# An accuracy check moved from steps 4–9 to steps 11–15 of the first blocks, and a row-placing product with four matmuls in place of eight

## The chip, the cores and the metric

One NeuronCore of a Trainium2 chip runs the whole kernel in one launch. The metric is device time in microseconds (us) of that core. Five engines work side by side, each through its own list of instructions in the order of the program: TensorE (PE; its weight loads are shown apart as PEld), VectorE (DVE), ScalarE (ACT), GpSimd (POOL) and SyncE (SP), which here only issues transfers. An instruction that has to wait for another engine holds up everything behind it on its own engine.

## The reference

The output is the sum of the input, a Fourier mixing and a token-mixing MLP, both fed by a layer norm:

```python
xn = _layernorm(x, axis=-1)
return x + _A_ref(xn, dft_seq_re, dft_seq_im, dft_hid_re, dft_hid_im) + _B_ref(xn, w1, b1, w2, b2)
# A: y = Cr @ (xn @ Dr^T) - Ci @ (xn @ Di^T)      Cr, Ci 2048x2048; Dr, Di 640x640
# B: u = gelu(h^T @ w1 + b1), y = (u @ w2 + b2)^T  h = layernorm(xn); w1 2048x1728, w2 1728x2048
```

There are 2048 tokens and 640 channels, all in float32. The Fourier matrices come as inputs; the kernel uses their symmetries to read and multiply only a part of them, so it also has to check that the matrices it was given have these symmetries. If a check fails, a general branch at the end computes everything again.

## The kernel before

**Arithmetic.** A float32 operand is split into a high part (rounded, written by ACT, function `high`, line 130) and a low part (what is left, written by DVE, function `low`, line 133). A product is then three matmuls: high by high, high by low, low by high (function `three`, lines 138 to 140). Nearly all matmuls move 320 columns against 128x128 weights.

**Steps.** The program is a list of steps, each with about 24 matmuls of 320 columns. At each step `i` the final loop (lines 1329 to 1343) emits, in this order: the loads of step `i`, the reads of finished sums, the high part of the weight piece of step `i+2`, the work in the list `middle`, the low part of that piece, the work in the list `behind`, and last the matmuls of step `i`. Since the order is written by hand (`tc.manual_schedule()`), this is the order on each engine.

**The first blocks** are steps 0 to 15 (`n_first = 16`). Step `j` multiplies one block of 128 tokens (a row of x, normalized) by the four weight pieces of its group; sums for the first four blocks of hidden features collect in all eight PSUM banks (line 301). For each row of x there is a chain that runs through three engines: moments on DVE (lines 200, 203), a reciprocal root `q` on ACT (line 225), four small operations on POOL (lines 229 to 232, tiles `r` and `again`), the normalized row on ACT (tile `zt`, line 245), its high part on ACT (tile `x`, line 130) and its low part on DVE (tile `x`, line 133). In steps 4 to 11 ACT and DVE also cut the weight pieces 8 to 15 (tile `early`).

**Around step 16.** In step 14 DVE writes the low part of the last row, then four 0/1 matrices (`places_compare`, lines 415 and 417), then the low part of the weight piece of step 16 (tile `piece`). In step 15 ACT cuts the piece of step 17, computes `q_all` (line 398) and loads the table for gelu (line 1161); DVE computes the factors of all rows (lines 399 to 402), splits them (`norm_parts`, tile `norm_cut`), checks two scales (`scale_check`, lines 1103 to 1107) and writes the low part of the piece of step 17. At the head of step 16 ACT reads the eight banks with gelu (line 325, eight instructions, banks 0 and 1 first). The matmuls of step 16 write into banks 0 and 1 and cannot begin before these were read.

**The check sets.** A set (`seq_set`, `set_at`) loads four pieces of 512 KB of the sequence matrices: a base and three ends. Three ends are compared with the base on DVE (end 1: line 999; end 2: line 1003 twice; end 3: line 1005 twice) and the base with its own mirror image (line 1012). Each of the four differences is squared and summed on ACT right after it (line 1022, `measure`, which for early sets is emitted with the compare). The list `when` holds the steps of the four loads; a compare follows its load by `by` steps, in the list `behind`. Seven sets are early (they load through SP); the first of them is the one that moves. Its loads stand at steps 4, 4, 5, 6 and its compares at steps 7, 8 and 9. Its base lies in the tile `ck0`, which `scale_load` (lines 1097 and 1098, step 10) also uses; its ends lie in the memory of the tiles `n6` and `n7`, which later hold the last four rows of x.

**The factors' places.** Step 17 ends with `norm_products`: 0/1 matrices bring the factors of the rows, their high and low part one after the other, into the order that the Fourier part wants (line 429, eight matmuls of 32 columns into bank 6). In step 18 `norm_places` copies the sums with ACT (line 436) into `ck1`, and POOL spreads them (lines 443 to 448) into `norm_pairs`, first used in step 20 (line 470).

Of the kernel before, what the change touches and what calls it, by code (L numbers as in the profile page):

```python
# [8 lines left out]
F32 = mybir.dt.float32  # L9
# [3 lines left out]
AF = mybir.ActivationFunctionType  # L13
# [3 lines left out]
P = 128  # L17
S = 2048
D = 640
F = 1728  # L20
NS = S // P
# [28 lines left out]
def fnet_plus_mixer(  # L50
# [22 lines left out]
    nc = tc.nc  # L73

    keep = ctx.enter_context(tc.tile_pool(name="keep", bufs=1))
# [28 lines left out]
    norm_cut = keep.tile([P, 2, NS, 2], R32, name="norm_cut")  # L104
# [18 lines left out]
    psum = [acc.tile([P, CH], F32, name=f"psum{i}") for i in range(8)]  # L123
    idle = nc.const_aps.tensor(1.0, [P, CH], dtype=BF16)
    for i in range(WARM):
        n = CH if i < WARM - 8 else P // 2
# [18 lines left out]
    def at(i, f, *args, when=middle):  # L145
        when[i].append(lambda: f(*args))
# [188 lines left out]
    for f, g in up_order:  # L335

        def products(w, f=f, g=g):
            for k in range(g * G, (g + 1) * G):
                up_products(f, k, w, up_banks[f])
            if (f, g) == (FIRST, 1):  # L340
                norm_products()

        at(len(steps) - 6, w1_load, f, g, when=loads)
        top, bottom = cut_view(lambda a: a[:, :CH], lambda f=f, g=g: w_at[f, g])

        def beside(top=top, f=f, g=g):
            hi = top_tiles[f, g]
            pieces = [a.rearrange("p (k t) -> p k t", k=G)[:, :, TAIL:] for a in (hi, w_at[f, g])]
            low(pieces[0], pieces[1], pieces[0])
            return hi, hi  # L350

        def top_beside(f=f, g=g):
            top_tiles[f, g] = cut_tile()[:, 0, :CH]
            high(top_tiles[f, g], w_at[f, g])

        steps.append(((top, bottom) if f < NF else (top_beside, beside)) + (products,))
        if g == NG - 1 and f < NF:
            at(len(steps) + (f == NFB - 2), gelu, f, when=reads)
# [60 lines left out]
    lanes_of, places = [], []  # L419
# [3 lines left out]
        low(norm_cut[:, 1], norm, norm_cut[:, 0])  # L423

    def norm_products():
        n = 2 * NS
        for c in range(4):
            for part in range(2):
                nc.tensor.matmul(
                    psum[6][:, c * n : (c + 1) * n], places[0][:, c // 2, c % 2], norm_cut[:, part].rearrange("p k c -> p (k c)"),  # L430
                    start=c == 0 and part == 0, stop=c == 3 and part == 1, skip_group_check=True,
                )

    def norm_places():
        of = ck[1][:, : 8 * NS]
        nc.scalar.activation(of, psum[6][:, : 8 * NS], AF.Copy)
        of = of.rearrange("p (s v h k c) -> p s v h k c", s=2, v=2, h=2, k=HS)
        to = norm_pairs.rearrange("p (h b j v) c -> p b v h j c", h=2, b=2, v=2)
        half = P // 2
        for v in range(2):  # L440
            for i in range(2):
                p = slice(half * i, half * (i + 1))
                nc.gpsimd.tensor_copy(to[p, 0, v], of[p, 0, v, :, i : i + 2 * NJ - 1 : 2])

            nc.gpsimd.tensor_copy(to[:, 1, v], of[:, 1, v, :, HS - 2 : HS - 1 - 2 * NJ : -2])
            p = slice(0, half + 1 - v)
            nc.gpsimd.tensor_copy(to[p, 1, v], of[p, 1, v, :, HS - 1 : HS - 2 * NJ : -2])
        nc.gpsimd.tensor_copy(to[0:1, 1, 0], of[0:1, 1, 0, :, NK : NK + 2 * NJ - 1 : 2])
# [582 lines left out]
    def set_at(u, when, by, base, places, late):  # L1031
        load, compare, compare_mirror = seq_set(u, base, places, late)
        for i in range(len(when)):
            at(when[i], load, i, when=loads)
            if i:
                at(when[i] + by, compare, i, when[i] + by, when=behind)
        at(when[-1] + by, compare_mirror, when[-1] + by, when=behind)
# [88 lines left out]
    n_first = len(k_order)  # L1126
# [24 lines left out]
    at(n_first - 2, places_compare)  # L1151
    at(n_first - 1, norm_parts)
    at(n_first + 2, norm_places)
    for j in range(NJ):
        for h in range(2):
# [6 lines left out]
    for k in range(HS):  # L1162
        i = n_first + 3 + 4 * k
# [6 lines left out]
    i = n_first + 3 + 4 * NK  # L1170
# [8 lines left out]
    sets = [m * HS + k for m in range(2) for k in range(NG, HS)] + [m * HS + k for m in range(2) for k in range(NG)]  # L1179

    def early_base(n):
        return lambda: ck[(n + 1) % 2][:, : S // 2]
# [4 lines left out]
        return keep.tile([P, S // 2], F32, name=f"check{n}", tag=f"h{4 + i}")  # L1187


    first_ends = []  # L1190

    def first_place(i):
        if i != 1:
            first_ends.append(keep.tile([P, 2, S // 2], F32, name=f"check_first{i}", tag=f"n{6 + i // 2}"))
        return first_ends[-1][:, i % 2]

    set_at(sets[0], [4, 4, 5, 6], 3, early_base(1), first_place, 0)
    for n in range(1, n_early):
        i = n_first + 4 * (n - 1)
        when = [i, i, i + 1, i + 2] if n < n_early - 1 else [i, i, i + 1, i + 4]  # L1200
# [20 lines left out]
    for n in range(n_hid_units):  # L1221
        load, compare, compare_own, measure = hid_unit(n)
        i = begin + 4 + 8 * n
# [256 lines left out]
```

## Time and profile before

| what | value |
|---|---|
| median of 3 runs | 439.84 us (439.14 to 439.93) |
| the profiled execution | 439.92 us, span of its instructions 438.1 us |
| TensorE busy | 430.7 us, 98% of the span, 2963 matmuls |
| VectorE busy | 326.1 us, 74% |
| ScalarE busy | 247.1 us, 56% |
| GpSimd busy | 108.6 us, 25% |
| mean granted TensorE clock | 0.997 |
| HBM | 94.58 MB read, 10.49 MB written |

The span runs from the first instruction to the last. What lies between 438.1 and 439.92 us is outside the instructions. A row of the timeline gives start and duration in us, the engine, the line of the kernel, the operation, the tile written and the tiles read, and in square brackets how long the engine sat idle before and what ended it. Ends of matmuls are modelled: a matmul of 320 columns is drawn 0.31 us long, while the next one starts after some 0.15 us.

### The profile page before, as it was taken

The page shows a single profiled execution, that of the slowest core. Times are in us where ns is not written, and L with a number is a line of the kernel's source. Part 1 is how long each engine was busy: PE and PEld are TensorE (multiplying, and loading weights), DVE is VectorE, ACT ScalarE, POOL GpSimd, SP SyncE. Part 2 cuts the span into 40 slices and gives each one's busy share as a digit, 9 for nine tenths or more (in the row PEclk, how much of TensorE's full clock was granted, in tenths as well). Part 3 has the DMA queues.
Part 4 walks back from the last instruction along what each step waited for, and adds up shares of the span by engine and source line. Part 5 has one row for each costly group of instructions (what it writes and reads, how often), then busy time and mean ns, then how long its engine had stood idle before and what let it go on. Part 6 is the DMA issues. An engine that isn't in the chain of part 4 may idle for free.

```text
span 438.1 us, 8076 instructions
## 1 busy us (share of the span) xinstructions
PE 430.7 (98%) x2963; PEld 424.4 (97%) x2963; DVE 326.1 (74%) x665; ACT 247.1 (56%) x476; POOL 108.6 (25%) x164
## 2 busy tenths in 40 slices
PE   9999999999999999999999999999999999999994
PEld 5999999999999999999999999999999999999994
DVE  7887861578777777795888759989778677869671
ACT  5967955566556646475946424556645555545540
POOL 2056511032220001100002425546434516312000
PEclk9999999999999999999999999999999999999998
DMA  8992347597886561233203799999999988996301
GB/s 271 339 373 101 104 180 272 178 322 269 279 287 226 194 222 57 72 99 95 101 23 122 212 339 397 389 396 364 404 402 399 399 315 287 407 328 240 113 31 38
DMA packets 43839, 105.68 MB, mean 241 GB/s; under 512 B 5748, under 2 KB 7940, under 8 KB 43792
## 3 DMA queue, kind: packets, MB, share of 16 engines
q1 hardware_dynamic: 34816, 72.66, 46.5%
q0 software_dynamic: 8832, 32.27, 20.2%
q8 instruction: 25, 0.41, 0.4%
q14 instruction: 22, 0.18, 0.1%
q10 hardware_dynamic: 144, 0.16, 0.1%
HBM read 94.58 MB, written 10.49 MB: 240 GB/s over the span
## 4 chain that ended last, share of the span: by engine, by line
PE 87%; DMA 3%; DVE 3%; ACT 2%; POOL 2%; issue 1%; SPq 1%; POOLq 0%; ACTq 0%
PE psum L138 26%; PE psum L140 26%; PE psum L139 26%; PE psum L301 4%; PE psum L897 2%; PE psum L290 2%; DMA xp<-in_x 1%; ACT zt L245 1%; DMA xm<-in_x 1%; POOL r L230 1%; DVE st L200 1%; DVE x L133 1%; DVE early L133 0%; SPq L1258 0%; ACT x L130 0%
## 5 line engine op out<-in xcount | busy, mean ns | idle before, releaser
L133 DVE TENSOR_TENSOR piece<-w_raw,piece 128x512 fp32r<-128x512 f32 (+2 forms) x128 | 76.5, 598 | 80.3 <-ACT piece L130 75.6
L130 ACT ACTIVATE piece<-w_raw 128x512 fp32r<-128x512 f32 (+2 forms) x112 | 67.0, 600 | 110.1 <-PE psum L140 73.4
L138 PE MATMUL psum<-x,piece 128*128 128x320 f32 x288 | 89.1, 309 | 0.0
L140 PE MATMUL psum<-x,piece 128*128 128x320 f32 x288 | 89.1, 309 | 0.0
L139 PE MATMUL psum<-x,piece 128*128 128x320 f32 x288 | 88.8, 308 | 0.0
L1022 ACT ACTIVATE check<-check 128x1024 f32<-128x1024 f32 (+2 forms) x62 | 61.4, 991 | 32.5 <-DVE check L1005 14.2
L140 PE MATMUL psum<-h_cut,piece 128*128 128x320 f32 x256 | 79.2, 310 | 0.0
L138 PE MATMUL psum<-h_cut,piece 128*128 128x320 f32 x256 | 79.1, 309 | 0.0
L139 PE MATMUL psum<-h_cut,piece 128*128 128x320 f32 x256 | 78.8, 308 | 0.0
L301 PE MATMUL psum<-x,early 128*128 128x320 f32 x384 | 58.5, 312 | 1.1 <-DVE x L133 0.4
L301 PEld LDWEIGHTS psum<-x,early 128*128 128x128 f32 x384 | 56.4, 188 | 3.1 <-ACT x L130 1.2
L138 PEld LDWEIGHTS psum<-x,piece 128*128 128x128 f32 x288 | 54.1, 188 | 0.0
L139 PEld LDWEIGHTS psum<-x,piece 128*128 128x128 f32 x288 | 54.1, 188 | 0.0
L140 PEld LDWEIGHTS psum<-x,piece 128*128 128x128 f32 x288 | 54.1, 188 | 0.0
L138 PE MATMUL psum<-h_high,piece 128*128 128x320 f32 x160 | 49.6, 310 | 0.0
L139 PE MATMUL psum<-h_low,piece 128*128 128x320 f32 x160 | 49.4, 309 | 0.0
L140 PE MATMUL psum<-h_high,piece 128*128 128x320 f32 x160 | 49.3, 308 | 0.0
L139 PEld LDWEIGHTS psum<-h_cut,piece 128*128 128x128 f32 x256 | 48.1, 188 | 0.0
L140 PEld LDWEIGHTS psum<-h_cut,piece 128*128 128x128 f32 x256 | 48.1, 188 | 0.0
L138 PEld LDWEIGHTS psum<-h_cut,piece 128*128 128x128 f32 x256 | 48.1, 188 | 0.0
L991 POOL DMA_DIRECT2D check<-in_dft_seq x36 | 26.6, 744 | 16.8 <-ACT check L1022 15.5
L984 POOL DMA_INDIRECT check<-in_dft_seq,from_seq x16 | 19.1, 1191 | 44.8 <-ACT check L1022 41.8
(235 smaller groups left out, 781.7 us busy)
## 6 DMA issues: line engine op xcount, KB each, us to landing
check<-in_dft_seq POOLq DMA_DIRECT2D x36, 512.0 KB
w_raw<-in_w SPq DMA_DIRECT2D x56, 256.0 KB
check<-in_dft_seq SPq DMA_DIRECT2D x18, 512.0 KB
w_raw<-in_w SPq DMA_DIRECT2D x16, 512.0 KB
w_raw<-in_w SPq DMA_DIRECT2D x16, 384.0 KB
rest<-y SPq DMA_DIRECT2D x16, 320.0 KB
rest<-in_x SPq DMA_DIRECT2D x16, 320.0 KB
out<-rest SPq DMA_DIRECT2D x15, 320.0 KB
```

What stands on the lines that cost most here:

```text
L130: nc.scalar.activation(hi, src, AF.Copy)
L133: nc.vector.tensor_sub(lo, src, hi.bitcast(F32))
L138: nc.tensor.matmul(bank, wh, mh, start=first, stop=False, skip_group_check=True)
L139: nc.tensor.matmul(bank, wh, ml, start=False, stop=False, skip_group_check=True)
L140: nc.tensor.matmul(bank, wl, mh, start=False, stop=last, skip_group_check=True)
L200: nc.vector.bn_stats(stats[k][:, i, :], rows[k][:, i * H2 : (i + 1) * H2])
L290: nc.tensor.matmul(to[half][:, :H2], w[0][:, c], m[i], start=k == to[2] and i == 0, stop=k == to[3] and i == 1, skip_group_check=True,)
L301: nc.tensor.matmul(up_banks[f][half][:, :H2], w_cut[f, k // G][part == 2][:, c], n[:, part == 1, k % 2, half * H2 : (half + 1) * H2], star ...
L897: nc.tensor.matmul(to, w[0][:, c], m[which], start=False, stop=last and which == 1, skip_group_check=True,)
L984: nc.gpsimd.indirect_dma_start(to[:, c * CH : (c + 1) * CH], None, dft_seq.rearrange("c k p t -> (c k p) t"), bass.IndirectOffsetOnAxis(ap ...
L991: (nc.gpsimd if late else nc.sync).dma_start(to.rearrange("p (c t) -> p c t", c=2), dft_seq[c : c + 2, k + HS * (i // 2)].rearrange("c p t ...
L1022: nc.scalar.activation(v, v, AF.Square, accum_out=off[:, n : n + 1])
```

## The change

The check set that ran in steps 4 to 9 now loads in steps 11, 12, 12 and 13 (`n_first - 5`, `- 4`, `- 4`, `- 3`) and compares two steps later: ends 1 and 2 in step 14, end 3 and the mirror in step 15. Its base lies in `ck1` instead of `ck0`, its ends in the memory of `h0`, `h1` and `h2`, which until step 11 hold the weight pieces 8, 9 and 10 and after step 16 the outputs of gelu. In `norm_products` the high and low parts lie side by side, so that four matmuls of 64 columns do what eight of 32 did, and the sum of the two parts, which TensorE formed before by adding into the same columns, is formed in `norm_places`: ACT copies the low sums, and DVE adds the high sums to them.

```diff
     def norm_products():
-        n = 2 * NS
+        n = 4 * NS
         for c in range(4):
-            for part in range(2):
-                nc.tensor.matmul(
-                    psum[6][:, c * n : (c + 1) * n], places[0][:, c // 2, c % 2], norm_cut[:, part].rearrange("p k c -> p (k c)"),
-                    start=c == 0 and part == 0, stop=c == 3 and part == 1, skip_group_check=True,
-                )
+            nc.tensor.matmul(
+                psum[6][:, c * n : (c + 1) * n], places[0][:, c // 2, c % 2], norm_cut.rearrange("p i k c -> p (i k c)"),
+                start=c == 0, stop=c == 3, skip_group_check=True,
+            )
 
     def norm_places():
         of = ck[1][:, : 8 * NS]
-        nc.scalar.activation(of, psum[6][:, : 8 * NS], AF.Copy)
+        both = psum[6][:, : 16 * NS].rearrange("p (s i n) -> p i s n", s=4, i=2)
+        sums = of.rearrange("p (s n) -> p s n", s=4)
+        nc.scalar.activation(sums, both[:, 1], AF.Copy)
+        nc.vector.tensor_add(sums, both[:, 0], sums)
...
-    first_ends = []
-
     def first_place(i):
-        if i != 1:
-            first_ends.append(keep.tile([P, 2, S // 2], F32, name=f"check_first{i}", tag=f"n{6 + i // 2}"))
-        return first_ends[-1][:, i % 2]
-
-    set_at(sets[0], [4, 4, 5, 6], 3, early_base(1), first_place, 0)
+        return keep.tile([P, S // 2], F32, name="check_first", tag=f"h{i}")
+
+    set_at(sets[0], [n_first - 5, n_first - 4, n_first - 4, n_first - 3], 2, early_base(0), first_place, 0)
```

## The prediction

> **What bounds the kernel now.** I read the page first, for the share of each engine and the chain that ended last:
>
> ```profile
> PE 430.7 (98%) x2963; PEld 424.4 (97%) x2963; DVE 326.1 (74%) x665; ACT 247.1 (56%) x476; POOL 108.6 (25%) x164
> PE 87%; DMA 3%; DVE 3%; ACT 2%; POOL 2%; issue 1%; SPq 1%; POOLq 0%; ACTq 0%
> ```
>
> TensorE is the bound. So a change can do two things: shorten TensorE's list, or shorten or lengthen its gaps. Next I read TensorE's own timeline, for the gaps:
>
> ```profile
> 40.36 0.56 PE L301 MATMUL psum<-x,early 128*128 128x320 f32 x2 [0.18 <-DVE early L133]
> 41.26 8.48 PE L301 MATMUL psum<-x,early 128*128 128x320 f32 x56 [0.34 <-ACT x L130]
> 50.12 16.69 PE L301 MATMUL psum<-x,early 128*128 128x320 f32 x112 [0.38 <-DVE x L133]
> 66.65 0.31 PE L138 MATMUL psum<-x,piece 128*128 128x320 f32 x1
> ```
>
> From 50.12 to 66.65 run 112 matmuls without a gap, 0.148 us each; the last of these rows is the first matmul of step 16. At this pace the gaps ahead of the first three rows cost 0.18 + 0.31 - 0.15 = 0.34 us (the drawn end is 0.31 after a start), 0.90 - 0.30 = 0.60 (two matmuls take 0.90) and 8.86 - 8.27 = 0.59 (56 matmuls take 8.86): **1.53 us** in steps 8 to 11. The list of waits shows no gap of TensorE behind a work engine after that.
>
> Then the timeline of the other engines around these gaps:
>
> ```profile
> 33.02 0.28 ACT L225 ACTIVATE q<-mv,eps 128x1 f32<-128x1 f32 x1
> 34.95 0.92 ACT L245 ACTIVATE zt<-xp,again 128x640 f32<-128x640 f32 x1 [1.13 <-POOL again L232]
> ...
> 36.55 0.28 ACT L225 ACTIVATE q<-mv,eps 128x1 f32<-128x1 f32 x1
> 37.00 1.76 POOL L230 TENSOR_SCALAR r<-r,q 128x1 f32<-128x1 f32 x1 [1.37 <-ACT q L225]
> 37.42 1.29 DVE L999 SCALAR_TENSOR_TENSOR check_first<-ck,parity,check_first 128x1024 f32<-128x1024 f32 x1
> 39.52 0.92 ACT L245 ACTIVATE zt<-xp,again 128x640 f32<-128x640 f32 x1 [1.99 <-POOL again L232]
> ...
> 41.12 1.05 ACT L1022 ACTIVATE check_first<-check_first 128x1024 f32<-128x1024 f32 x1
> 41.99 1.29 DVE L1003 TENSOR_TENSOR check_first<-ck,check_first 128x512 f32<-128x512 f32 x2
> 42.16 0.62 ACT L130 ACTIVATE early<-w_raw 128x512 fp32r<-128x512 f32 x1
> ...
> 45.53 1.41 DVE L1005 SCALAR_TENSOR_TENSOR check_first<-ck,parity,check_first 128x512 f32<-128x512 f32 x2
> 46.98 0.75 DVE L1012 SCALAR_TENSOR_TENSOR ck<-ck,parity 128x512 f32<-128x512 f32 x1
> ...
> 48.82 0.62 ACT L1022 ACTIVATE ck<-ck 128x512 f32<-128x512 f32 x1
> ...
> 50.14 0.91 ACT L245 ACTIVATE zt<-xm,again 128x640 f32<-128x640 f32 x1
> ```
>
> The old place of the check makes those gaps. GpSimd's line 230 ends at 38.76, just as VectorE's compare of end 1 ends at 38.71, so the root-to-row path takes 39.52 - 36.55 = 2.97 us against 34.95 - 33.02 = 1.93 one row earlier: 1.04 us late. After that ScalarE's squares and VectorE's compares stand in the rows' chains.
>
> Last, the stretch in which the check lands:
>
> ```profile
> 58.51 1.14 ACT L130 ACTIVATE piece<-w_raw 128x512 fp32r<-128x512 f32 x2
> 59.38 0.22 DVE L415 TENSOR_SCALAR lane<-lane 128x128 int32<-128x128 int32 x1
> 59.55 0.29 ACT L398 ACTIVATE q_all<-mv,eps 128x16 f32<-128x16 f32 x1
> 59.86 1.28 ACT L1161 ACT_TABLE_LOAD   x1
> 60.51 0.68 DVE L133 TENSOR_TENSOR piece<-w_raw,piece 128x512 fp32r<-128x512 f32 x1
> 61.12 0.17 DVE L399 SCALAR_TENSOR_TENSOR r_all<-mv,q_all 128x16 f32<-128x16 f32 x1
> 63.98 0.67 DVE L133 TENSOR_TENSOR piece<-w_raw,piece 128x512 fp32r<-128x512 f32 x1
> 65.83 3.46 ACT L325 ACTIVATE h<-psum,b_sb 128x320 f32<-128x320 f32 x8 [4.47 <-PE psum L301]
> ```
>
> ScalarE waits 4.47 us for TensorE before the gelu reads, then TensorE starts step 16 0.82 us after the first of them begins. There is no slack on TensorE's side: if ScalarE is not free when step 15 ends, step 16 starts late and all that follows with it.
>
> **The check leaves steps 7 to 9.** TensorE's 1.53 us would go, so that step 16 could start at 66.65 - 1.53 = 65.12. The rows gain more. The row of 39.52 comes at 36.55 + 1.93 = 38.48, 1.04 us earlier. The three squares of the ends (42.16 - 41.12 = 1.04 each) and that of the mirror (0.62) leave ScalarE, another 3.74, and the ScalarE rows from 39.52 to 50.14 show no wait for anything else. So the row of 50.14 comes 4.78 us earlier, at 45.36. GpSimd hardly limits this: its factors must be there at 45.36, and its own chain, some 1.9 us after a root (as above), is shorter than ScalarE's 2.3 us a row ((10.62 - 3.74) / 3). From there to 59.38 nothing of the old check is left, so I move it as a block: VectorE reaches the 0/1 matrices at 59.38 - 4.78 = **54.60**.
>
> **The check arrives in steps 14 and 15.** I follow the hand-written order. VectorE: matrices 1.13 (60.51 - 59.38), low piece 0.61 (61.12 - 60.51), so end 1 begins at 56.34; end 1 takes 1.29 and end 2 1.29, to 58.92. ScalarE may not cut the piece of step 17 before it has squared end 2: 1.04, to 59.96; the piece 0.52 (half of 59.55 - 58.51), `q_all` 0.29, to 60.77. VectorE waits 1.85 us for that, since its next work needs `q_all`. Then come factors, split and scale check, 2.86 (63.98 - 61.12), the low piece 0.67, end 3 1.41: 65.71. ScalarE squares end 3 (1.04) and the mirror (0.62; the mirror's 0.75 on VectorE lies beside the square): **67.37**. The table load of 1.28 lies in ScalarE's wait. Only then gelu reads bank 0. Eight reads in 3.46 are 0.43 apart, and the start of step 16 lay 0.82 behind the first where TensorE set it; I take 0.60, between. Step 16 starts at 67.97 in place of 66.65: **+1.32 us**, though 65.12 was open to TensorE. The old wait goes, and a later one of 2.85 us comes; behind the gelu reads on ScalarE stand the pieces of steps 18 and 19, not due before 75.
>
> Bounds: drawn durations overlap a little (the piece of 60.51 lasts 0.68, its follower starts after 0.61), over eight instructions up to 0.6 us earlier; the hand-over may be 0.17 shorter (one read) or 0.22 longer (0.82); GpSimd may hold a row up by some 0.5. So +0.5 to +2.0.
>
> **Its four loads** of 512 KB leave SP's steps 4 to 6. No gap names a transfer there, so their leaving counts nothing; it cannot cost. In the new place ends 1 and 2 wait on SP until TensorE has left the weight pieces 8 and 9, near the end of step 11 (65.12 less four steps of 24 x 0.148 is 50.95; say 50.3). Queued behind them are the pieces of step 19 and later and the first pair loads, not due for 15 us.
>
> ```profile
> 49.83 1.77 SPq L267 DMA_DIRECT2D w_raw<-in_w  x4
> 51.50:52.00 0.50, 1.00 1.05 397
> ```
>
> Transfers issued at 49.83 flow in full (397 GB/s, last number of the window's row) 1.7 us later; 0.52 MB then take 1.3. Ends 1 and 2 land near 53.3 and 54.7, before 56.34 and 57.63: no cost. Only if they landed over 2.9 us later would the check slip by the rest. `scale_load` no longer waits for the base, since that is now `ck1`; nothing waited for it.
>
> **The factors' places.** TensorE first:
>
> ```profile
> 73.54 0.31 PE L140 MATMUL psum<-x,piece 128*128 128x320 f32 x1
> 73.68 0.96 PE L429 MATMUL psum<-norm_cut,places_of 128*128 128x32 f32 x8
> ...
> 74.72 0.31 PE L139 MATMUL psum<-x,piece 128*128 128x320 f32 x1
> ...
> 221.47 0.27 PE L139 MATMUL psum<-hid_main,t 128*128 128x162 f32 x1
> ...
> 222.03 0.35 PE L138 MATMUL psum<-hid_mix,t 128*128 128x324 f32 x1
> ```
>
> Between 73.54 and 74.72 lie the eight and two common matmuls: 1.18 - 0.30 = 0.88, or 0.11 each. From 221.47 to 222.03 five matmuls of 162 columns start, also 0.11 each. So 32 and 162 columns cost the same here, and 64 lie between: four instead of eight save **0.44** (0.40 to 0.48 with the rounding of the starts). In step 18 one copy on ScalarE stays a copy, and VectorE gets an addition that waits for it:
>
> ```profile
> 74.59 0.69 DVE L133 TENSOR_TENSOR piece<-w_raw,piece 128x512 fp32r<-128x512 f32 x1 [2.87 <-ACT piece L130]
> 74.68 0.28 ACT L436 ACTIVATE ck<-psum 128x128 f32<-128x128 f32 x1
> ```
>
> Queued behind the addition is the low part of step 20's piece, which now begins at 74.59. It waits for a copy that starts at 74.68 and an addition of 128 columns, which lasts between nothing and the 0.69 of the 512 columns above: at most 1.1 us later, and TensorE wants it two steps, 7.1 us, after. GpSimd's copies move by the addition too; their result is first used in step 20. I cost it at nothing.
>
> **Sum.** 439.92 (the profiled execution, 0.08 above the median of the runs) + 1.32 - 0.44 = **440.80 us**, with its own range 440.0 to 441.5. The gaps taken out of steps 8 to 11 come back, larger, in front of step 16.
>
> **The gap and the clock.** In the forecast TensorE idles from about 65.3 to 67.97, 2.7 us. What such a gap does to its clock the end and the beginning of the trace show:
>
> ```profile
> 432.32 0.31 PE L897 MATMUL psum<-h_low,piece 128*128 128x320 f32 x1
> ...
> 435.00:435.50 0.50, 0.00 (x0) 0.70 0.09 24
> ...
> 1.16 0.15 PEld L127 LDWEIGHTS <-const-bfloat16-1.0 128*128 128x128 bf16 x1 [0.27 <-issue]
> ...
> 5.00 2.10 PEld L127 LDWEIGHTS <-const-bfloat16-1.0 128*128 128x128 bf16 x15 [0.28 <-issue]
> ```
>
> The last matmul ends at 432.63; in the window from 435.0 the granted clock is 0.70 in the mean, so it fell from full to half near 435.2, 2.6 us after the end. That is as long as the forecast gap. At the start nine matmuls of 512 columns lie from 1.16 to 5.00, 0.43 apart, where 0.148 per 320 columns would make 0.24: 1.8 times slower for 3.8 us. [...]
>
> **The rivals.**
> *The clock falls in the gap.* Then step 16 begins slow: 3.8 us at 1.8 times lose 3.8 x (1 - 1/1.8) = 1.7, and the time is 442.5. For it: the 2.6 us above. Against: a gap of 2.7 is only just as long, and nothing shows that the fall always comes so early.
> *The check fits after all (faster).* Place: ScalarE at the head of step 16. If the mirror's square ends before 65.12 - 0.82 = 64.30, TensorE keeps its 1.53 and the 0.44: 437.95. For it: ScalarE's 4.47 us of idle time there and 4.78 us gained. Against: VectorE's list alone from 54.60 to the end of end 3, without any wait, is 1.13 + 0.61 + 1.29 + 1.29 + 2.86 + 0.67 + 1.41 = 9.26, so 63.86, and with the two squares 65.52; the limit is 1.2 us under this bare list.
> *The two halves cancel.* If the chain is about 1 us shorter than laid out (overlaps, and rows that gain more than 4.78 because GpSimd meets fewer VectorE instructions), step 16 starts near 66.9 and the time is 439.8, no change.
> *The change does not do what it says.* Four matmuls of 64 columns could cost as much as eight of 32; then the main case is 441.2. The equal price of 32 and 162 columns speaks against it.
>
> **How the numbers follow.** The main case has 0.50, the clock 0.25, the cancelling case 0.15, the fitting check 0.10; the fourth rival lies inside the main case's range. The predicted time is the main case's, 440.8. The range goes from 439.0, which takes in the cancelling case, to 442.7, just above the clock; it leaves out the fitting check and a tenth at the edges. A measurement of this kernel tells about 0.2% from no change, that is 0.88 us; so no change reaches to 440.72 and cuts the main case in two. Slower: the clock 0.25 and 0.30 of the main case, 0.55. No change: 0.20 of it and 0.12 of the cancelling case, 0.32. Faster: 0.13.
>
> **What would show it.** Right: TensorE has no gaps left between 40 and 65; the first gelu read begins near 67.4 and is released by ScalarE's own square, not by TensorE; TensorE's gap ahead of line 138's first matmul is 2 to 3 us; `q_all` comes behind the square of end 2 and VectorE idles near 1.9 us for it; line 429 has four matmuls about 0.11 apart. Wrong: gelu still waits for TensorE there (the check fits), the ends' compares wait for a transfer, or a granted clock under 1 after 68 (the clock).

## The result, and the profile after

The changed kernel takes 444.3 us (median of 4 runs, 444.13 to 445.22), the kernel before beside it 439.88 us (439.14 to 440.81): 1.0105 times as long, 95% interval 1.0092 to 1.0118. It is 4.4 us slower. The prediction was 440.8 us with a range of 439.0 to 442.7: the sign was right, the size was not.

The page of the profiled execution after (444.13 us, span 442.3 us; 4.2 us more than before in both): the busy time of TensorE and the number of its matmuls, the chain that ended last, and the granted clock in 40 slices of 11.06 us.

```profile
PE 430.9 (97%) x2959; PEld 425.1 (96%) x2959; DVE 326.6 (74%) x666; ACT 247.2 (56%) x476; POOL 108.0 (24%) x164
...
PEclk9999998999999999999999999999999999999998
...
PE 93%; ACT 2%; DMA 1%; issue 1%; SPq 1%; DVE 0%; ACTq 0%
```

Four matmuls fewer, the same busy time, and, besides the last slice, in which TensorE is done, one slice with a lower clock: the seventh, from 66.3 us. TensorE's timeline shows what happened there (line numbers behind line 437 are 2 higher than before: line 1022 is now 1024, 897 is 899; the norm products moved from 429 to 428).

```profile
7.01 57.80 PE L301 MATMUL psum<-x,early 128*128 128x320 f32 x384
69.11 0.41 PE L138 MATMUL psum<-x,piece 128*128 128x320 f32 x1 [4.30 <-ACT h L325]
...
77.65 0.31 PE L140 MATMUL psum<-x,piece 128*128 128x320 f32 x1
77.79 0.53 PE L428 MATMUL psum<-norm_cut,places_of 128*128 128x64 f32 x4
78.15 0.39 PE L138 MATMUL psum<-x,piece 128*128 128x320 f32 x1
78.39 0.31 PE L139 MATMUL psum<-x,piece 128*128 128x320 f32 x1
...
435.76 0.30 PE L899 MATMUL psum<-h_low,piece 128*128 128x320 f32 x1
...
436.68 0.38 ACTq L924 DMA_DIRECT2D out<-rest  x1
```

The gaps of steps 8 to 11 are gone: all 384 matmuls of the first blocks now stand in one row of the timeline, ending at 64.81. Then TensorE idles 4.30 us for the gelu reads, and step 16 starts at 69.11 instead of 66.65. From there the 4.2 us can be followed along the same points in both traces:

| stretch on TensorE | before, us | after, us | difference |
|---|---|---|---|
| span start to first matmul of step 16 | 66.65 | 69.11 | +2.46 |
| from there to the last common matmul ahead of the norm products | 6.89 (to 73.54) | 8.54 (to 77.65) | +1.65 |
| from that over the norm products to the second common matmul | 1.18 (to 74.72) | 0.74 (to 78.39) | -0.44 |
| from there to the last matmul | 357.60 (to 432.32) | 357.37 (to 435.76) | -0.23 |
| last matmul to the end of the span | 5.78 | 6.54 | +0.76 |

Why was step 16 late? First the rows of x, whose chain ends in the 0/1 matrices. The timeline of ScalarE, GpSimd and VectorE after, from 38 to 47 us (the rows of the three engines are set one engine after the other):

```profile
38.16 0.92 ACT L245 ACTIVATE zt<-xp,again 128x640 f32<-128x640 f32 x1 [0.93 <-POOL again L232]
...
42.57 0.28 ACT L225 ACTIVATE q<-mv,eps 128x1 f32<-128x1 f32 x1
43.14 0.92 ACT L245 ACTIVATE zt<-xp,again 128x640 f32<-128x640 f32 x1 [0.29 <-POOL again L232]
...
46.13 0.92 ACT L245 ACTIVATE zt<-xm,again 128x640 f32<-128x640 f32 x1 [0.60 <-POOL again L232]
...
41.67 1.44 POOL L232 TENSOR_SCALAR again<-mv,again 128x1 f32<-128x1 f32 x1
...
43.87 0.85 POOL L230 TENSOR_SCALAR r<-r,q 128x1 f32<-128x1 f32 x1
44.81 0.93 POOL L231 TENSOR_SCALAR again<-r,q 128x1 f32<-128x1 f32 x1
...
41.67 0.65 DVE L133 TENSOR_TENSOR early<-w_raw,early 128x512 fp32r<-128x512 f32 x1
42.23 0.82 DVE L133 TENSOR_TENSOR x<-zt,x 128x640 fp32r<-128x640 f32 x1
...
44.01 0.65 DVE L133 TENSOR_TENSOR early<-w_raw,early 128x512 fp32r<-128x512 f32 x1
44.87 0.82 DVE L133 TENSOR_TENSOR x<-zt,x 128x640 fp32r<-128x640 f32 x1 [0.20 <-ACT x L130]
```

ScalarE, without the squares, waits for GpSimd ahead of each of these three rows (0.93, 0.29 and 0.60 us); of the rows in this stretch only the one at 40.47 comes without a wait. GpSimd's operations of lines 230 to 232, which take 0.26 to 0.34 us at 39 to 41 us, end 0.05 to 0.06 us after a low part on VectorE ends: the 1.44 us one at 43.11 (VectorE's second low part at 43.05), the two of 0.85 and 0.93 us at 44.72 and 45.74 (44.66 and 45.69). The root of 42.57 reaches its row at 46.13, 3.56 us later. In that time GpSimd also fills an index tile (line 409, 43.06 to 43.49); no run took this out, so its share is not known.

Then the stretch in which the check lands, VectorE and ScalarE after:

```profile
55.72 0.22 DVE L415 TENSOR_SCALAR lane<-lane 128x128 int32<-128x128 int32 x1
...
57.46 1.28 DVE L1001 SCALAR_TENSOR_TENSOR check_first<-ck,parity,check_first 128x1024 f32<-128x1024 f32 x1
58.66 1.29 DVE L1005 TENSOR_TENSOR check_first<-ck,check_first 128x512 f32<-128x512 f32 x2
61.93 0.18 DVE L399 SCALAR_TENSOR_TENSOR r_all<-mv,q_all 128x16 f32<-128x16 f32 x1 [1.99 <-ACT q_all L398]
...
65.40 1.40 DVE L1007 SCALAR_TENSOR_TENSOR check_first<-ck,parity,check_first 128x512 f32<-128x512 f32 x2
...
67.94 0.61 ACT L1024 ACTIVATE ck<-ck 128x512 f32<-128x512 f32 x1
...
68.55 3.43 ACT L325 ACTIVATE h<-psum,b_sb 128x320 f32<-128x320 f32 x8
```

The gelu reads stand directly behind ScalarE's own square of the mirror; before, they waited 4.47 us for TensorE.

Last, windows of half a microsecond after (window, its length, the busy time of TensorE, its weight loads, VectorE, ScalarE and GpSimd with the number of instructions, then granted clock, DMA share and GB/s):

```profile
69.50:70.00 0.50, 0.50 (x5) 0.50 (x4) 0.00 (x0) 0.50 (x2) 0.00 (x0) 0.86 0.78 205
70.00:70.50 0.50, 0.50 (x3) 0.50 (x3) 0.00 (x0) 0.50 (x2) 0.00 (x0) 0.50 0.82 291
...
72.50:73.00 0.50, 0.50 (x4) 0.50 (x3) 0.47 (x1) 0.00 (x0) 0.00 (x0) 0.50 1.08 418
73.00:73.50 0.50, 0.50 (x4) 0.50 (x4) 0.23 (x1) 0.00 (x0) 0.00 (x0) 0.73 1.04 397
```

A mean of 0.86 puts the fall from 1 to 0.50 at 69.86, 0.75 us after step 16 began, and 0.73 puts the return at 73.27: 3.41 us at half clock, with the matmuls 0.267 us apart instead of 0.147.

### The profile page after: what moved, and what is told of

It reads as the page before. It is cut to its first block, busy times and chain, and to the rows that moved or that the text cites. A ratio compares the mean times of both kernels' runs of the same rounds, so it can differ in the third digit from the quotient of the medians.

```text
span 442.3 us, 8075 instructions
## 1 busy us (share of the span) xinstructions
PE 430.9 (97%) x2959; PEld 425.1 (96%) x2959; DVE 326.6 (74%) x666; ACT 247.2 (56%) x476; POOL 108.0 (24%) x164
## 4 chain that ended last, share of the span: by engine, by line
PE 93%; ACT 2%; DMA 1%; issue 1%; SPq 1%; DVE 0%; ACTq 0%
PE psum L138 26%; PE psum L139 26%; PE psum L140 26%; PE psum L301 10%; PE psum L899 2%; PE psum L290 2%; DMA xp<-in_x 1%; ACT early L130 1%; SPq L1256 0%; ACT zt L245 0%; ACT ck L212 0%; ACT x L130 0%; ACT ck L218 0%; SPq L1248 0%; ACT x L245 0%
## 5 line engine op out<-in xcount | busy, mean ns | idle before, releaser
L138 PEld LDWEIGHTS psum<-x,piece 128*128 128x128 f32 x288 | 54.8, 190 | 4.6 <-ACT h L325 4.6
L140 PEld LDWEIGHTS psum<-x,piece 128*128 128x128 f32 x288 | 54.8, 190 | 0.0
L139 PEld LDWEIGHTS psum<-x,piece 128*128 128x128 f32 x288 | 54.7, 190 | 0.0
L138 PEld LDWEIGHTS psum<-h_high,piece 128*128 128x128 f32 x160 | 30.1, 188 | 0.0
```

What stands on the lines that cost most here:

```text
L138: nc.tensor.matmul(bank, wh, mh, start=first, stop=False, skip_group_check=True)
L139: nc.tensor.matmul(bank, wh, ml, start=False, stop=False, skip_group_check=True)
L140: nc.tensor.matmul(bank, wl, mh, start=False, stop=last, skip_group_check=True)
```

## The experiments

**The two halves alone.** The first kernel has the moved check and the old eight matmuls, the second the old check and the four matmuls.

```diff
 # the first: the lines of norm_products and norm_places stay as they were
+    set_at(sets[0], [n_first - 5, n_first - 4, n_first - 4, n_first - 3], 2, early_base(0), first_place, 0)
 # the second: this line stays as it was
     set_at(sets[0], [4, 4, 5, 6], 3, early_base(1), first_place, 0)
```

> Only the check set moves; the factors' places keep their eight matmuls. My theory (all of the loss comes from the check: ScalarE's squares stand ahead of gelu, and TensorE's clock falls in the gap): 444.3 + 0.44 = 444.7 us, gap ahead of step 16 near 4.3 us, granted clock half for about 3.4 us. Rival (the new addition on VectorE in step 18 holds up its queue and part of the loss is there): clearly under 444.3.

> Only the four matmuls of 64 columns with the addition on VectorE; the check set stays in steps 4 to 9. My theory: 439.88 - 0.44 = 439.44 us, TensorE without a gap after 66.6. Rival (the addition's wait for ScalarE costs): 440 us or more and a wait on VectorE that reaches TensorE in step 20.

The move alone: 444.98 us (444.3 to 446.26), 1.0121 times before (1.0103 to 1.0139). The norm products alone: 439.66 us (439.03 to 440.22), 0.9992 (0.9983 to 1.0), beside 440.11 us for the kernel before. The whole loss belongs to the move; it shows the same 4.30 us gap and the half clock. Between the same two matmuls the four take 0.44 us less, as the trace said, and no gap of TensorE follows from what VectorE adds now. In time the gain of 0.45 us stands at the edge of the noise, since the interval reaches 1.0.

**The check out of gelu's way.** The load of end 3 goes one step later, so that end 3 and the mirror are compared in step 16, behind the gelu reads. In a second kernel the set is left out; its time is that of a kernel that checks one set less.

```diff
-    set_at(sets[0], [n_first - 5, n_first - 4, n_first - 4, n_first - 3], 2, early_base(0), first_place, 0)
 # end 3 later:
+    set_at(sets[0], [n_first - 5, n_first - 4, n_first - 4, n_first - 2], 2, early_base(0), first_place, 0)
 # no first set: the line is left out
```

> The changed kernel with the last load one step later, so that end 3 and the mirror are compared and squared in step 16, behind the gelu reads; ends 1 and 2 stay in step 14. My theory: ScalarE is free at 63.4, gelu is released by TensorE again, no gap, the clock stays at 1.00; 439.9 - 1.5 - 0.44 = 438.0 us, faster than both kernels. Rival (the loss comes from elsewhere in steps 11 to 15, such as SP's wait for the weight pieces' memory or the row chain): still over 441 us with a gap ahead of step 16.

> The changed kernel without this one check set: its four loads, compares and squares are left out, so one of the sixteen symmetry checks is not made. My theory: 438.0 us, as with end 3 behind gelu, within 0.3. On the row chain: if GpSimd's factors limit the rows once the check is gone, the 0/1 matrices on VectorE begin near 55.7 as in the changed kernel; if ScalarE limits them at 2.3 us a row, as the prediction said, near 54.6.

End 3 later: 438.8 us (437.94 to 440.08, 12 runs), 0.9973 (0.9964 to 0.9982), which beats both kernels. Without the set: 437.99 us (437.73 to 438.21), 0.9953 (0.9939 to 0.9968). The rows of ScalarE and TensorE with end 3 later:

```profile
64.03 3.46 ACT L325 ACTIVATE h<-psum,b_sb 128x320 f32<-128x320 f32 x8 [0.44 <-ACT one L1163]
```

```profile
64.81 0.31 PE L138 MATMUL psum<-x,piece 128*128 128x320 f32 x1
```

Gelu now comes 0.44 us after ScalarE is done, TensorE has no gap ahead of step 16, and the clock stays at 1. So the place of end 3 and the mirror decides the sign of the whole change. The kernel without the set tells something else too. Its ScalarE:

```profile
38.98 0.92 ACT L245 ACTIVATE zt<-xp,again 128x640 f32<-128x640 f32 x1 [0.94 <-POOL again L232]
...
46.96 0.92 ACT L245 ACTIVATE zt<-xm,again 128x640 f32<-128x640 f32 x1 [0.60 <-POOL again L232]
...
64.66 3.46 ACT L325 ACTIVATE h<-psum,b_sb 128x320 f32<-128x320 f32 x8 [6.11 <-PE psum L301]
```

Three rows take 7.98 us, as in the changed kernel (46.13 - 38.16 = 7.97), though no instruction of the first check is left anywhere. The rows' pace is their own: from the first of them to the 0/1 matrices (38.98 to 56.56) pass 17.58 us, in the changed kernel 17.56 (38.16 to 55.72). ScalarE's idle time before gelu is 6.11 us: that is the space that the move wanted to use.

**Is it the clock?** TensorE is kept at work in the first 2.3 us of the gap by 36 matmuls that write a part of a bank that nobody reads (36 matmuls more than needed); the changed kernel itself runs beside it once more.

```diff
             for part in range(2 if j < 2 else 3):
                 up_pass(k, part)
+            if j == len(k_order) - 1:
+                for _ in range(36):
+                    nc.tensor.matmul(psum[7][:, H2 : H2 + P], idle[:, :P], idle[:, :P], start=True, stop=True, skip_group_check=True)
```

> The changed kernel itself, as the base of the next three on the same chip: 444.3 us, gap ahead of step 16 about 4.3 us, half clock for about 3.4 us somewhere after 66; if the fall sits on a free-running grid, it begins at another distance behind the last matmul than the 5.0 us of the first profile.

> The changed kernel with 36 matmuls of no use (bf16, 128 columns, into columns 320 to 447 of bank 7, which nothing reads) behind the matmuls of step 15, so that TensorE is busy for most of its wait. My theory: the gap costs the same, gelu begins at the same time, but the granted clock stays at 1.00, and the 1.5 us of the slow matmuls go: 442.8 us. Rival (the slow matmuls have another cause, such as the transfers that run at 70): no change, 444.3, with slow matmuls of 0.27 us apart still there.

The changed kernel again: 445.54 us (444.5 to 446.25), 1.0125 (1.0106 to 1.0144). With the matmuls in the gap: 443.58 us (443.08 to 444.54), 1.0088 (1.0071 to 1.0105): 1.96 us less, for more work. Its TensorE, and a window of it:

```profile
64.75 2.29 PE L317 MATMUL psum<-const-bfloat16-1.0 128*128 128x128 bf16 x36
69.22 0.42 PE L138 MATMUL psum<-x,piece 128*128 128x320 f32 x1 [2.17 <-ACT h L328]
...
76.37 0.53 PE L431 MATMUL psum<-norm_cut,places_of 128*128 128x64 f32 x4
```

```profile
70.00:70.50 0.50, 0.50 (x5) 0.50 (x4) 0.00 (x0) 0.50 (x2) 0.00 (x0) 1.00 0.97 307
```

Step 16 still starts late, at 69.22, but at full clock. From its start to the norm products pass 7.15 us, against 8.64 in the changed kernel beside it (69.43 to 78.07) and 7.03 before. So the fall of the clock costs 1.5 us; the start came 0.2 us earlier as well. The last 0.3 us of the 1.96 are less than what two executions of the changed kernel differ by: from the second common matmul behind the norm products to the last matmul they took 357.37 us (78.39 to 435.76) and 358.11 us (78.66 to 436.77). The idle 2.17 us behind the added matmuls did not cost the clock. The time is 0.8 us above the 442.8 that was expected.

**A shorter chain.** Ends 1 and 2 load one step later, so all compares stand in step 15, behind the scale check. Then VectorE does not wait for `q_all`, since ScalarE has no squares ahead of it.

```diff
-    set_at(sets[0], [n_first - 5, n_first - 4, n_first - 4, n_first - 3], 2, early_base(0), first_place, 0)
+    set_at(sets[0], [n_first - 5, n_first - 3, n_first - 3, n_first - 3], 2, early_base(0), first_place, 0)
```

> The changed kernel with the loads of ends 1 and 2 one step later, so that all compares stand in step 15 behind q_all and the scale check. My theory (VectorE's 2.0 us of idle time for q_all, which waits behind the square of end 2, is in the path): gelu begins 2.0 us earlier, near 66.5, the gap is near 2.3 us; 442.3 us if the clock falls, 440.8 if it does not. Rival (the sum of VectorE's work sets the end, the wait is only shifted): no change in the start of gelu, 444.3.

Measured: 441.74 us (440.81 to 443.49, 7 runs), 1.0043 (1.0027 to 1.006). From the 0/1 matrices (56.62) to gelu pass 10.75 us in place of 12.83, and no wait for `q_all` is left:

```profile
56.62 0.22 DVE L415 TENSOR_SCALAR lane<-lane 128x128 int32<-128x128 int32 x1
...
67.37 3.02 ACT L325 ACTIVATE h<-psum,b_sb 128x320 f32<-128x320 f32 x7
```

```profile
67.93 0.41 PE L138 MATMUL psum<-x,piece 128*128 128x320 f32 x1 [2.22 <-ACT h L325]
```

The gap of 2.22 us kept the clock at 1. Gelu came at 67.37 and not near 66.5, as expected, since this execution reached the matrices 0.9 us later than the first of the changed kernel. So here a shorter stall is worth more than its length: the first 2.1 us taken from the gap brought 3.8 us beside the changed kernel (445.54 - 441.74). That the clock held is in part luck, by the estimate of the last section; the slowest of the seven runs, at 443.49 us, has a mean granted clock of 0.991, the others 0.995 to 0.999. It has no trace; a lost clock there is likely, not shown.

**Do VectorE's low parts hold GpSimd?** Of the rows from step 7 on, the second half of the moments is moved behind the low part of the weight piece, so that it stands between the two low parts that ran back to back.

```diff
-            at(j, moments, k_order[n], when=reads)
+            if j < 7:
+                at(j, moments, k_order[n], when=reads)
+            else:
+                at(j, half_moments, k_order[n], 0, when=reads)
+                at(j, half_moments, k_order[n], 1, when=behind)
+                at(j, joined, k_order[n], when=behind)
```

> The changed kernel with the moments of the last five rows split in halves, so that on VectorE the low part of a weight piece and the low part of a row no longer follow each other directly. My theory (the rows from 38 to 46 come 1.1 us later than the prediction's 2.3 us a row because GpSimd's small operations are held up for as long as two VectorE instructions with two inputs run back to back): GpSimd's longest one falls from 1.44 to under 0.9 us, the three rows take 0.5 to 1.1 us less, gelu begins as much earlier: 443.2 to 443.8 us. Rival (ScalarE's own list or the wait for the roots sets the rows): no change, 444.3.

Measured: 445.25 us (444.88 to 446.38), 1.0127 (1.011 to 1.0144): no gain in time, where 443.2 to 443.8 had been expected. The rows:

```profile
35.88 0.92 ACT L245 ACTIVATE zt<-xp,again 128x640 f32<-128x640 f32 x1 [1.67 <-POOL again L232]
39.95 0.92 ACT L245 ACTIVATE zt<-xp,again 128x640 f32<-128x640 f32 x1 [1.49 <-POOL again L232]
...
47.28 0.92 ACT L245 ACTIVATE zt<-xm,again 128x640 f32<-128x640 f32 x1 [0.34 <-POOL again L232]
...
38.75 0.67 DVE L133 TENSOR_TENSOR early<-w_raw,early 128x512 fp32r<-128x512 f32 x1
...
38.75 0.81 POOL L231 TENSOR_SCALAR again<-r,q 128x1 f32<-128x1 f32 x1
```

The three rows that the edit was made for take 7.33 us instead of 7.97, and GpSimd's longest operation there 0.90 us instead of 1.44: as expected if VectorE's low parts hold it. From there to the 0/1 matrices everything follows 1.0 us sooner (39.95 to 56.51 is 16.56, before the edit 17.56). But the row ahead of them takes 4.07 us (35.88 to 39.95) where the changed kernel takes 3.53 (34.63 to 38.16), and so does the one before it (31.81 to 35.88, against 31.10 to 34.63): 1.08 us lost ahead of the 1.0 us won. In both, the low part of the weight piece now comes earlier on VectorE, behind half of the moments, and meets GpSimd's line 231: it takes 0.81 us, from 34.68 and from 38.75, against 0.27 and 0.26 in the changed kernel, and that is the whole 0.54 us of each row. The matrices come 0.79 us later than in the changed kernel; the other 0.7 of it stood already between the rows of 23.80 and 24.50 of the two executions, ahead of the edit. So the new order moved the meetings of GpSimd with the low parts from some rows to others, and their lengths account for what was lost. That supports the cause, but it is no cure.

**Both changes with end 3 later, and the end of the span.** The span ends 5.62 us after the last output transfer is issued in the changed kernel (436.68 to 442.3), 4.85 before (433.25 to 438.1). In every kernel with the set in the new steps and the four matmuls this end was 5.6 to 5.95 us, in all others 4.6 to 5.0. So I ran the set with end 3 later and the eight matmuls, beside the one with four.

```diff
     set_at(sets[0], [n_first - 5, n_first - 4, n_first - 4, n_first - 2], 2, early_base(0), first_place, 0)
 # and norm_products, norm_places as in the kernel before
```

> The check set moved with end 3 and the mirror behind the gelu reads (its last load one step later), and the factors' places with the old eight matmuls. What the moved check gains is then without the four matmuls. Every profile of a kernel that has both the moved set and the four matmuls ends 5.6 to 5.95 us after its last output transfer is issued, every other one 4.6 to 5.0. Theory A (the longer end belongs to the combination, wherever it comes from): this kernel has eight matmuls, 0.44 us more of TensorE, but the short end, 0.8 us less: about 438.4 us. Theory B (the longer end goes with the moved set and has nothing to do with the four matmuls, and the one old-norm run with it was chance): 438.8 + 0.44 = 439.2 us. In both the first matmul of step 16 follows the last of step 15 without a gap over 0.5 us and the granted clock stays 1.

> The kernel with end 3 and the mirror behind the gelu reads and four matmuls, once more beside the one with eight. 438.8 us again; its end after the last output transfer's issue again near 5.7 us if the longer end belongs to the program, near 4.9 if it was chance of one execution.

With eight matmuls: 438.2 us (438.14 to 438.3); with four: 438.21 us (437.99 to 439.01); both 0.9962 (0.9949 to 0.9976) of the kernel before, which took 439.8 us there. From step 16's start over the norm products to the next matmul pass 7.84 us with eight (65.14 to 72.98) and 7.40 with four (65.55 to 72.95), again 0.44. But the end takes 4.99 us with eight (431.51 to 436.5) and 5.62 with four (431.48 to 437.1). So the longer end belongs to the program, not to one execution, and it takes the four matmuls' gain back. The trace also holds SyncE's semaphore instructions, which the timeline leaves out, and they show where the time lies: after the last output transfer is issued, SyncE's closing series of them begins 3.35 to 3.67 us later in the seven kernels with the longer end, and 2.35 to 2.71 us later in the five others; from there to the end pass 2.2 to 2.6 us in all twelve. What SyncE waits for before this series stays open.

## Why the prediction was wrong, point by point

The time follows from the prediction's own sum by four differences: 440.80 + 1.12 (0/1 matrices later) + 1.65 (half clock behind the gap) - 0.23 (the long stretch behind) + 0.76 (the end) = 444.10; the chain and the hand-over add 0.02, and the rest to 444.13 is rounding. The largest is the clock, which the main case put at nothing; with it alone the time would be 442.45, inside the range. The late rows and the longer end took it out of the range.

*The check leaves steps 7 to 9:* right that TensorE's gaps there go. Wrong in size: the three rows were to take 6.88 us, 2.3 each, and took 7.97. **The step that failed is "GpSimd hardly limits this".** It compared GpSimd's chain of 1.93 us, read at one row where little of VectorE's work fell on it (line 230 took 0.72 us there, against 0.34 at 38.94 after the change), with ScalarE's pace, and took it as fixed. With ScalarE faster, GpSimd's operations meet VectorE's low parts (1.44, 0.85 and 0.93 us in place of 0.26 to 0.34), the root's way to its row becomes 3.56 us, and ScalarE waits. The kernel without any first set has the same pace, so it is not the check that holds them in the new place. The matrices came at 55.72 instead of 54.60: 1.09 us from these rows and 0.35 from the rows behind (46.13 to 55.72 is 9.59, moved as a block of 9.24), less 0.32 by which this execution was early at its first row (38.16, forecast 38.48). What the trace shows of the meeting is how close the two ends lie: three times a GpSimd operation ended 0.05 to 0.06 us after a low part. With two low parts in a row both outcomes occur: the 1.44 us operation ended after the second (it ends at 43.11, the low parts at 42.32 and 43.05), one of 0.92 us at 47.81 after the first (it ends at 48.73, the low parts at 48.68 and 49.28). By what means a low part holds GpSimd up, no run shows.

*The check arrives in steps 14 and 15:* right, nearly to the row. The matrices to gelu were laid out as 12.77 us and took 12.83; VectorE's wait for `q_all` as 1.85 and was 1.99; the hand-over from gelu to TensorE as 0.60 and was 0.56. Gelu is released by ScalarE's own square, as said. Its loads were issued from 49.88 and no compare waited for one.

*The factors' places:* right, -0.44 us on TensorE, alone and beside the move. The added wait on VectorE cost TensorE nothing. Here are the rows after:

```profile
78.87 0.29 DVE L438 TENSOR_TENSOR ck<-psum,ck 128x128 f32<-128x128 f32 x1 [3.04 <-ACT ck L437]
79.08 0.68 DVE L133 TENSOR_TENSOR piece<-w_raw,piece 128x512 fp32r<-128x512 f32 x1
```

*The gap and the clock:* the fall was there as a rival with a chance of 0.25 and a price of 1.7 us; it came, and cost 1.5 of the 1.65 us by the kernel with work in the gap. It was held less likely because the gap was forecast at 2.7 us, only just as long as the 2.6 us after which the clock fell at the end of the trace before. That the clock holds over such a gap, on which the 440.80 counts, was the author's estimate; no run shows it. The gap was 4.30, since the rows were late by 1.12 and TensorE, without its gaps, was done 0.5 us earlier than forecast (its last matmul is drawn to 64.81, forecast about 65.3). The two errors were not independent: the late rows lengthened the gap, and the gap of 4.30 us lost the clock where one of 2.22 us kept it. The chance of 0.25 was too low even for 2.7 us: by the bounds of the last section such a gap loses the clock at 54% to 82% of the places where it can lie (an estimate from these traces: at 54% of them 2.13 us or more of the gap lie in one interval of 3.41 us, at 82% 1.65 us or more). The range took in the clock on top of the main sum, but not the clock on top of late rows. In the traces gaps of 4.30 us and 3.29 us (the kernel with split moments) lost the clock, gaps of 2.22 and 2.17 did not. By the estimate of the last section the length alone does not decide it.

*That the check fits after all, and that the halves cancel:* neither came. The first needed ScalarE free by 64.30; it was free at 68.55. With end 3 later it is free early enough, and the time is 438.2 to 438.8 against the 437.95 that the rival named.

*The end of the span* was taken as unchanged; it became 0.76 us longer. No step of the prediction spoke of it.

## What to carry to other kernels

When a block of work leaves a chain, look for the next limit of that chain at its new pace, not at a place where the old one gave it room: here GpSimd's small operations took back 1.1 of the 4.8 us that the rows were to gain. Work in front of a hand-over between engines is best cut where its last consumer stands: the same change costs 4.4 us with the check's last two compares ahead of the gelu reads and gains 1.3 to 1.6 us with them behind. And price a forecast gap of TensorE together with its clock: here 2.1 us less of it brought 3.8 us, in an execution whose 2.22 us gap kept the clock at 1.

## What the runs showed of the hardware

In these traces the fall of the clock has no fixed delay. In the four traces in which the half clock came back (the changed kernel twice, the move alone, the split moments) it lasted 3.41 us. But over all traces the clock fell between 2.1 and 5.1 us after the end of the last matmul ahead of the idle time. The nearest pair is at the end of the two kernels of the last comparison, whose last matmuls end at 430.89 and 430.85. With eight matmuls:

```profile
432.50:433.00 0.50, 0.00 (x0) 0.00 (x0) 0.00 (x0) 0.00 (x0) 0.00 (x0) 1.00 0.82 249
433.00:433.50 0.50, 0.00 (x0) 0.00 (x0) 0.00 (x0) 0.00 (x0) 0.00 (x0) 0.53 0.17 55
```

With four:

```profile
434.50:435.00 0.50, 0.00 (x0) 0.00 (x0) 0.00 (x0) 0.00 (x0) 0.00 (x0) 1.00 0.00 0
435.00:435.50 0.50, 0.00 (x0) 0.00 (x0) 0.00 (x0) 0.00 (x0) 0.00 (x0) 0.77 0.13 33
```

The one falls at 433.03, 2.1 us after its last matmul, the other at 435.27, 4.4 us after. In the changed kernel the clock fell 5.05 us after the last matmul (64.81 to 69.86), when TensorE had been at work again for 0.75 us; when it was run again, 4.24 us after (65.13 to 69.37). Another distance than the first is what its expectation named as the sign of a free-running grid.

The traces record each change of the granted clock: in the kernel before, to full at 5.12 us and to half at 435.20; in the changed kernel, to full at 5.01, to half at 69.86, to full at 73.27 and to half at 438.50. Here are the lengths of the stretches that lie between two changes, counted from the change to full clock with which each record opens:

| stretch, us | in intervals of 3.4133 us | where |
|---|---|---|
| 3.41 | 1 | half clock in the four traces named above |
| 64.85 | 19 | from the opening to the fall behind the gap, the same four |
| 365.23 | 107 | from the return to the fall at the end, the changed kernel |
| 368.64 | 108 | the same, in the other three of the four |
| 426.67 | 125 | end 3 later (first run); the same with eight matmuls |
| 430.08 | 126 | before; norm products alone; no set; compares in step 15; end 3 later (again) |
| 433.49 | 127 | the kernel with work in the gap |

Each is a whole number of intervals to within 0.01 us. So in these traces the changes of the clock lie on a grid of 3.4133 us (430.079 / 126). The grid is not tied to the start of the program: the opening change lies anywhere from 3.48 to 6.77 us after the start of the span.

Counted in these intervals, with the matmuls as long as they are drawn, the intervals that end in a fall stand apart from the others in these traces. All sixteen falls come at the end of an interval with 0 to 1.28 us of matmuls in it; no interval at full clock with 1.76 us or more ends in a fall, and no interval at full clock lies between the two figures. The gap of the changed kernel puts 1.64 us of idle time into one interval and 2.66 into the next, and the clock falls behind the second. The gap of 2.22 us lay over a boundary, 1.48 and 0.74 us, and that of 2.17 too, 1.28 and 0.89. In one interval, either would have left 1.2 us of work (3.41 less the gap), less than the 1.28 behind which the clock fell. No run placed a gap on purpose; by these bounds (an estimate) a gap under 1.6 us keeps the clock (3.41 - 1.76 = 1.65), one over 4.3 us loses it (2 x (3.41 - 1.28) = 4.26), and between them its place in the grid takes part in the decision.
